# A gated unit beside attention on one core: how the two row halves of TensorE swap their halves of h

## The chip, the cores and the metric

One core of a Trainium2 chip. A kernel's time is the device time of one execution in microseconds (us); what is compared is the median over several executions. The engines are TensorE (PE, with its weight loads shown as PEld), VectorE (DVE), ScalarE (ACT), GpSimd (POOL) and SyncE (SP). In this kernel SP does nothing but issue DMA transfers, in the order in which the program hands them to it. A PE matmul writes its sums to PSUM, in banks of 128 x 512 float32; everything else lies in SBUF, 128 partitions wide.

## The reference

x has 2048 rows of 576. Attention with 32 heads of 18 columns, times the silu of a bilinear gated unit with F = 4608 inner columns, plus x:

```python
xn  = layernorm(x)                       # (2048, 576)
q, k, v = heads(xn @ wqkv)               # 32 heads, Dh = 18
p   = softmax(q @ k.T * Dh ** -0.5)      # per head, 2048 x 2048
s   = merge(p @ v) @ wo
h   = (xn @ w_gate) * (xn @ w_up)        # (2048, 4608)
g   = silu(h @ w_down)
out = x + s * g
```

All of it is float32. Where the kernel needs more than one pass of the array gives, a number is split in a high part (rounded to the type that PE multiplies fast, float32r) and a low part (the number less its high part), and a product takes three matmuls: high x high, high x low, low x high.

## The kernel before

A prologue (to about 194 us) normalises x and makes q, k and v. An end (from about 2502 us) multiplies by wo and writes the output. Between them lies the main stage, of which the change touches a part.

**Two streams on two halves of the array.** In the main stage the 128 rows of PE's array are used as two halves of 64 rows, and two matmuls that name different halves run beside each other. Stream 0 (rows 0 to 63) and stream 1 (rows 64 to 127) each hand out matmuls of the gated unit; scores of the attention are put between them, and the products with v (L639, float32, the whole array) come in 74 "visits", each of which stops both streams. Two passes are made over the scores: pass a (L596) for the row maximum, which DVE takes (L598), and pass b (L628), whose scores ACT turns into exponentials `pt` (L630). Pass b has two PSUM banks, `pb`. Pass a has two, `pa`. The unit and the visits share four, `pg`.

**The gated unit** is cut into 72 units u = (c, q): c is one of four chunks of 512 rows of x, q one of 18 groups of 256 inner columns. The 18 units of a chunk are called a sweep here. A unit has two products j = 0, 1 of 128 columns each, numbered n = 2u + j. Stream 0 computes up (27 matmuls of 512 columns, L675) and ACT copies it to SBUF (`us`, L680, in `up_end`). Stream 1 computes gate, and DVE multiplies the two in `gate_end` (L687): `us` now holds h of 128 inner columns for 512 rows. ACT rounds it to the high part `hs` (L690), POOL takes the low part (L691).

**The exchange.** The down product of the unit sums over 256 inner columns: each stream makes one half of the 576 output columns and needs all inner columns, but a stream's matmuls read only the 64 partitions of their own half. So each half needs the other half's h on its own partitions: `turn_round` moves the parts `hs` of one half to the partitions of the other, as `hx`, with two DMAs of 512 KB for a unit (L709). Then down takes 4 blocks of 128 rows, each 12 matmuls of 288 columns (L719, in the order of `DTERMS`: for j = 0 three with `hs` and three with `hx`, then the same for j = 1), and DVE adds the block to `acc` (L747, in `down_end`). `hx` has one buffer: the exchange for unit u+1 can only be issued when the last L719 of unit u has read `hx`. `down_end` does that when both streams have ended the unit: it calls `d_get(u + 1)`, which loads or prepares the next down weights, and then `turn_round(u + 1, 1)`. For unit 0 and the last two units `gate_end` calls `turn_round` itself; there the last unit but one has a buffer of its own, `hxl`.

**The weights.** In the first sweep they come from memory as they are, and are split on the way: "chores" round a piece on ACT (L193 for the gate and up weights `wgu`, L226 for the down weights `wd`), take the low part on POOL (L194, L227), store the split tile for later (L199, L232, 1152 KB each) and issue the loads of the raw weights ahead (L116, L124). In the later sweeps `wgu` and `wd` are loaded ready split (L185, L220, 1152 KB each). SP also issues the loads of q and k (L245, `ring` and `pair`), of v (L584) and, at the end, of the attention rows (o<-sot).

**What sets the order.** The program is unrolled, and a planner (`order`) writes it out when the kernel is built. It keeps a clock for each stream and times at which DVE, ACT and POOL come free; `can_go` says if a stream's next matmul may go, by the tables `there`, `downed`, `loaded`, `upped` and `gated`. `moved(start, size)` estimates when a transfer of so many MB lands, as one queue of 0.24 MB/us plus 2.0 us. Every engine's instructions then run on the chip in the order in which the planner wrote them, and an instruction that has to wait holds up all that stand behind it on its engine.

## Time and profile before

| | before |
|---|---|
| median of 3 runs | 2568.7 us (2567.2 to 2570.92) |
| the profiled execution's own time | 2567.59 us |
| its span in the profile | 2565.8 us |
| L675, gate and up matmuls | 7776, of 388 ns |
| L596 and L628, scores on half arrays | 2006 and 2005, of 393 and 395 ns |
| L630, exponentials on ACT | 2048, of 597 ns |

The profile shows one execution. Its times are in us from the span's start. A row of the list of groups names the line, the engine, the operation, what is written and read, the count, then the busy sum and the mean duration of one in ns. Matmuls on the two half arrays overlap, so their durations add to more than the span. A row of the waits names who waited on whom, then the sum, the count and the longest. A row of the timeline begins with the start and the duration; in square brackets stands how long the engine had been idle, and what ended it. SPq is the time that SP takes to issue a DMA. A row of the table of stretches gives the stretch, its length and the busy time (with the number of instructions) of PE, PEld, DVE, ACT, POOL and SPq, then the mean granted clock, the busy share of the DMA engines, and GB/s.

### The profile page before, as it was taken

Reading aid. Unit: us, or ns where it says so; the run is one execution under the profiler, and the core shown is the slowest. Engines: PE = TensorE matmul, PEld = TensorE weight load, DVE = VectorE, ACT = ScalarE, POOL = GpSimd, SP = SyncE. Lnnn points to the kernel's source line nnn. Section 1 sums busy time; section 2 is a strip of 40 time slices with the busy share of each in tenths; the row PEclk is TensorE's granted clock in tenths of the full one; section 3 lists DMA queues with packets and bytes.
Section 4 is the critical chain, followed back from the end, with each engine's and each line's share of the span. In section 5 each row is a group of like instructions: output and inputs, shape, how many; then the busy total and the mean of one; then the engine's idle time right before and its main releaser. Section 6 shows DMA issues by size and latency. Waiting matters only on the chain.

```text
span 2565.8 us, 59206 instructions
## 1 busy us (share of the span) xinstructions
PE 2544.8 (99%) x24360; PEld 2106.5 (82%) x24360; DVE 1931.5 (75%) x3377; ACT 1465.2 (57%) x2688; POOL 593.3 (23%) x663
## 2 busy tenths in 40 slices
PE   8999999999999999999999999999999999999999
PEld 7899888878878888878888888887888888878879
DVE  6208778777778898777778888777888887877537
ACT  5222666666756665655565666555665655555651
POOL 3214334433421111111111111111111111111125
PEclk9999999999999999999999999999999999999999
DMA  7799988888886666565676666665676666664577
GB/s 248 233 283 279 259 227 226 233 222 224 221 193 187 176 180 180 172 182 168 181 186 171 179 175 185 179 166 169 180 192 166 178 184 178 175 177 145 154 203 253
DMA packets 196058, 504.58 MB, mean 197 GB/s; under 512 B 58144, under 2 KB 116384, under 8 KB 156876
## 3 DMA queue, kind: packets, MB, share of 16 engines
q1 hardware_dynamic: 185100, 487.58, 68.2%
q0 software_dynamic: 9952, 11.74, 1.7%
q8 instruction: 192, 3.15, 0.6%
q10 hardware_dynamic: 736, 1.47, 0.2%
q14 instruction: 78, 0.64, 0.1%
HBM read 312.21 MB, written 107.61 MB: 164 GB/s over the span
## 4 chain that ended last, share of the span: by engine, by line
PE 97%; DVE 1%; DMA 1%; SPq 0%; issue 0%; ACT 0%; POOL 0%; DVEq 0%
PE pg L675 34%; PE pg L639 17%; PE pg L719 16%; PE pa L596 12%; PE pb L628 8%; PE pg L402 2%; PE pa L348 2%; PE pb L348 2%; PE pg L1243 1%; PE pa L1243 1%; PE pb L1243 1%; DMA hx<-hs 0%; DMA ring<-sqk 0%; DVE mx L598 0%; DMA xin<-in_A_x_dram 0%; DMA sot<-oc 0%
## 5 line engine op out<-in xcount | busy, mean ns | idle before, releaser
L598 DVE TENSOR_REDUCE mx<-pa 128x1 f32<-128x512 f32 x2048 | 1368.9, 687 | 226.1 <-PE pa L596 113.1
L630 ACT ACTIVATE pt<-pb 128x512 f32<-128x512 f32 x2048 | 1160.8, 597 | 538.2 <-PE pb L628 463.5
L675 PE MATMUL pg<-xc,wgu 64*128 64x512 f32 x7776 | 1363.9, 388 | 0.2 <-DVE acc L747 0.2
L675 PEld LDWEIGHTS pg<-xc,wgu 64*128 64x128 f32 x7776 | 1049.4, 184 | 41.4 <-DVE acc L747 0.5
L628 PE MATMUL pb<-pair,ring 64*128 64x512 f32 x2005 | 780.8, 395 | 2.3 <-DMA ring<-sqk 2.3
L596 PE MATMUL pa<-pair,ring 64*128 64x512 f32 x2006 | 777.3, 393 | 1.8 <-DVE mx L598 1.8
L719 PE MATMUL pg<-wd,hs 64*128 64x288 f32 x3408 | 585.1, 293 | 2.4 <-DVE acc L747 2.4
L719 PE MATMUL pg<-wd,hx 64*128 64x288 f32 x3360 | 572.4, 293 | 2.0 <-DMA hx<-hs 2.0
L719 PEld LDWEIGHTS pg<-wd,hs 64*128 64x128 f32 x3408 | 491.8, 185 | 7.1 <-DVE acc L747 2.8
L691 POOL TENSOR_TENSOR hs<-us,hs 128x512 fp32r<-128x512 f32 x144 | 185.9, 1291 | 1315.7 <-ACT hs L690 1301.6
L719 PEld LDWEIGHTS pg<-wd,hx 64*128 64x128 f32 x3360 | 480.4, 185 | 5.6 <-DMA hx<-hs 2.3
L639 PE MATMUL pg<-pt,vt 128*32 128x512 f32 x4096 | 455.8, 595 | 0.8 <-DVE acc L747 0.6
L596 PEld LDWEIGHTS pa<-pair,ring 64*128 64x128 f32 x2006 | 364.8, 184 | 70.7 <-issue 52.8
L628 PEld LDWEIGHTS pb<-pair,ring 64*128 64x128 f32 x2005 | 364.2, 184 | 9.3 <-issue 2.7
L639 PEld LDWEIGHTS pg<-pt,vt 128*32 128x32 f32 x4096 | 125.6, 110 | 285.1 <-issue 280.0
L747 DVE TENSOR_TENSOR acc<-acc,pg 128x288 f32<-128x288 f32 x544 | 234.0, 446 | 21.1 <-PE pg L719 20.1
L645 DVE TENSOR_TENSOR oc<-oc,pg 128x512 f32<-128x512 f32 x69 | 47.1, 683 | 216.6 <-PE pg L639 213.0
L690 ACT ACTIVATE hs<-us 128x512 fp32r<-128x512 f32 x144 | 91.0, 632 | 149.6 <-DVE us L687 148.0
L194 POOL TENSOR_TENSOR wgu<-wraw,wgu 128x384 fp32r<-128x384 f32 x108 | 108.4, 1015 | 97.3 <-ACT wgu L193 81.3
L643 ACT ACTIVATE oc<-pg 128x512 f32<-128x512 f32 x32 | 19.1, 598 | 184.9 <-PE pg L639 184.9
L687 DVE TENSOR_TENSOR us<-pg,us 128x512 f32<-128x512 f32 x144 | 98.4, 683 | 29.0 <-PE pg L675 22.3
L618 POOL DMA_DIRECT2D pair<-mt x128 | 77.6, 612 | 166.6 <-DVE mt L613 162.5
(143 smaller groups left out, 1366.5 us busy)
## 6 DMA issues: line engine op xcount, KB each, us to landing
wgu<-swg SPq DMA_DIRECT2D x102, 1152.0 KB
hx<-hs SPq DMA_DIRECT2D x140, 512.0 KB
wd<-swd SPq DMA_DIRECT2D x50, 1152.0 KB
swg<-wgu SPq DMA_DIRECT2D x36, 1152.0 KB
pair<-sqk SPq DMA_DIRECT2D x192, 144.0 KB
ring<-sqk SPq DMA_DIRECT2D x384, 72.0 KB
swd<-wd SPq DMA_DIRECT2D x18, 1152.0 KB
sqk<-hl SPq DMA_DIRECT2D x32, 512.0 KB
```

The source lines that it names most:

```text
L194: nc.gpsimd.tensor_tensor(w[:, 9 + b:12 + b, :], raw[:, b:b + 3, :], w[:, b:b + 3, :].bitcast(FT), op=OP.subtract)
L348: nc.tensor.matmul(p, wq[b, a], xcs[c][:, e, :], start=n == 0, stop=n == len(PAIRS) - 1)
L596: nc.tensor.matmul(p, q[rows, t * 128:(t + 1) * 128], k[rows, c * 512:(c + 1) * 512], start=True, stop=True)
L598: nc.vector.tensor_reduce(mx[h][:, t, c:c + 1], p, axis=AX.X, op=OP.max)
L628: nc.tensor.matmul(p, k[rows, t * 128:(t + 1) * 128], q[rows, c * 512:(c + 1) * 512], start=True, stop=True)
L630: nc.scalar.activation(pt[t, c], p, AF.Exp, scale=scale)
L639: nc.tensor.matmul(p[32 * c:32 * c + 32, :], vt[h // 2][:, t, 6 * (h % 2):6 * (h % 2) + 32], pt[t, c], start=t == ts[0], stop=t == ts[-1])
L675: nc.tensor.matmul(ps, gw[n][half[r], a, :], xg[i][half[r], e, :], start=k == 0, stop=k == len(TERMS) - 1)
L687: nc.vector.tensor_tensor(h32, ps, h32, op=OP.mult)
L691: nc.gpsimd.tensor_tensor(hj[:, 1, :], h32, hj[:, 0, :].bitcast(FT), op=OP.subtract)
L719: nc.tensor.matmul(ps[:, 0:HALF], (hx if k else hs)[u][half[r], j, a, s * 128:(s + 1) * 128], dw[u][half[r], k, j, e, :], start=n == 0, st ...
L747: nc.vector.tensor_tensor(a, a, ps[:, 0:HALF], op=OP.add)
```

## The change

The exchange moves the float32 product instead of its two parts. `turn_round` now sends `us` itself, as one DMA of 128 KB for each j and each half (L707), into the place where the low part will stand. When it has landed, the new function `cross` rounds it on ACT to the high part (L711) and POOL replaces it by the low part (L712), the same two operations as L690 and L691. `down_end` calls `turn_round(u + 1, (0, 1))` ahead of `d_get(u + 1)` instead of behind it. In unit 0 and the last two units each j is sent by `gate_end`.

In the planner, `there["h", n]` (the whole exchange) becomes `there["h", n, j]`, and `there["o", n, j]` is added for a half's own h. `can_go` asks for each of the four parts where down begins to read it, where it asked for all of `hx` at the first matmul. `sent` is the time by which a product has left `us`, which an up product now also waits for. The list `crossing` holds each `cross` back until the estimated landing plus BEFORE (1.5 us) and until ACT is free. L719, L745 and L747 of the kernel before are L722, L748 and L750 in the changed one.

```diff
         def gate_end(n, ps):
...
-            h32 = us.pop(n)
+            h32 = whole_h[n] = us.pop(n)
             nc.vector.tensor_tensor(h32, ps, h32, op=OP.mult)
             g_get(n + 2)
             hj = hs[u][:, j]
             nc.scalar.activation(hj[:, 0, :], h32, AF.Copy)
             nc.gpsimd.tensor_tensor(hj[:, 1, :], h32, hj[:, 0, :].bitcast(FT), op=OP.subtract)
-            if u == 0 and j or u >= len(units) - 2:
-                turn_round(u, j)
+            if u == 0 or u >= len(units) - 2:
+                turn_round(u, (j,))
...
-        def turn_round(u, j):
+        def turn_round(u, js):
...
-            for r in range(2):
-                nc.sync.dma_start(hx[u][half[r], js].bitcast(FT), hs[u][half[1 - r], js].bitcast(FT))
+            for j in js:
+                h32 = whole_h.pop(2 * u + j)
+                for r in range(2):
+                    nc.sync.dma_start(hx[u][half[r], j, 1, :].bitcast(FT), h32[half[1 - r], :])
+
+        def cross(u, j):
+            high, low = hx[u][:, j, 0, :], hx[u][:, j, 1, :]
+            nc.scalar.activation(high, low.bitcast(FT), AF.Copy)
+            nc.gpsimd.tensor_tensor(low, low.bitcast(FT), high.bitcast(FT), op=OP.subtract)
...
+                    if u + 1 < len(units) - 2:
+                        turn_round(u + 1, (0, 1))
                     d_get(u + 1)
-                    if u + 1 < len(units) - 2:
-                        turn_round(u + 1, 1)
...
+        LATER, BEFORE = 0.5, 1.5
...
             if kind == "d":
-                return k or (there.get(("h", n), 1e9) <= now and (n < 1 or downed.get(n - 1, 1e9) <= now))
+                if k % 3 == 0 and k < 12:
+                    if there.get(("oh"[k // 3 % 2], n, k // 6), 1e9) > now:
+                        return False
+                return k or n < 1 or downed.get(n - 1, 1e9) <= now
...
+                if crossing and crossing[0][0] + max(0.0, free["ACT"] - now - 0.1) <= now:
+                    _, u, j = crossing.pop(0)
+                    cross(u, j)
+                    there["h", u, j] = engine("POOL", engine("ACT", now, 0.535) + 0.05, 1.29) + LATER
...
-                                    downed[n] = moved(max(parts[n]) + 0.3, 1.18) if (n + 1) % NF2 and n + 2 < len(units) else 0.0
                                     if n + 3 < len(units):
-                                        there["h", n + 1] = moved(max(parts[n]) + 1.0, 1.05)
+                                        for j in range(2):
+                                            sent[2 * n + 2 + j] = moved(max(parts[n]) + 0.3, 0.262)
+                                            crossing.append((sent[2 * n + 2 + j] + BEFORE, n + 1, j))
+                                    downed[n] = moved(max(parts[n]) + 1.0, 1.18) if (n + 1) % NF2 and n + 2 < len(units) else 0.0
...
```

Where this moves instructions, engine by engine. First SP in the first sweep, at the exchange that has the load of v ahead of it. Before:

```order
L199 DMA swg<-wgu 128x2304
L116 DMA wraw<-in_B_w_up_dram 64x9x128
L116 DMA wraw<-in_B_w_gate_dram 64x9x128
L584 DMA vt<-sv 128x16x38
L709 DMA hx<-hs 64x2048 x2
L232 DMA swd<-wd 128x2304
```

And now, at the same place:

```order
L199 DMA swg<-wgu 128x2304
L116 DMA wraw<-in_B_w_up_dram 64x9x128
L116 DMA wraw<-in_B_w_gate_dram 64x9x128
L584 DMA vt<-sv 128x16x38
L707 DMA hx<-us 64x512 x4
L232 DMA swd<-wd 128x2304
```

Two transfers have become four smaller ones, and what stands ahead of them is the same. ACT at that place, before:

```order
L226 ACTIVATE wd<-draw 128x2x288
L630 ACTIVATE pt<-pb 128x512 x2
L226 ACTIVATE wd<-draw 128x2x288
L630 ACTIVATE pt<-pb 128x512 x3
L680 ACTIVATE us<-pg 128x512
L630 ACTIVATE pt<-pb 128x512 x2
L690 ACTIVATE hs<-us 128x512
```

And now:

```order
L226 ACTIVATE wd<-draw 128x2x288
L630 ACTIVATE pt<-pb 128x512 x2
L226 ACTIVATE wd<-draw 128x2x288
L630 ACTIVATE pt<-pb 128x512 x2
L711 ACTIVATE hx<-hx 128x512
L630 ACTIVATE pt<-pb 128x512
L680 ACTIVATE us<-pg 128x512
L711 ACTIVATE hx<-hx 128x512
L630 ACTIVATE pt<-pb 128x512 x2
L690 ACTIVATE hs<-us 128x512
```

The two L711, one for each product j, stand between exponentials, one of them ahead of the copy of up. In a later sweep SP had the load of the next down weights (L220) ahead of the exchange:

```order
L245 DMA ring<-sqk 18x1024 x3
L584 DMA vt<-sv 128x16x38
L220 DMA wd<-swd 128x2304
L709 DMA hx<-hs 64x2048 x2
L185 DMA wgu<-swg 128x2304
```

And now:

```order
L245 DMA ring<-sqk 18x1024 x3
L584 DMA vt<-sv 128x16x38
L707 DMA hx<-us 64x512 x4
L220 DMA wd<-swd 128x2304
L185 DMA wgu<-swg 128x2304
```

The exchange has moved ahead of that load. Last, PE at the end of the main stage, from the last visit (L639) on. Before, where the names `hs` and `hxl` are a unit's own and exchanged parts of h:

```order
L639 MATMUL pg<-pt,vt 32x512 x16
L719 MATMUL pg<-wd,hxl 128x288 x5
L719 MATMUL pg<-wd,hs 128x288 x6
L719 MATMUL pg<-wd,hxl 128x288 x6
L719 MATMUL pg<-wd,hs 128x288 x6
```

And now, where `wdl` and `hx` belong to the last unit:

```order
L639 MATMUL pg<-pt,vt 32x512 x16
L722 MATMUL pg<-wd,hxl 128x288 x3
L722 MATMUL pg<-wd,hs 128x288 x3
L722 MATMUL pg<-wd,hxl 128x288 x3
L722 MATMUL pg<-wd,hs 128x288 x3
L722 MATMUL pg<-wd,hxl 128x288 x3
L722 MATMUL pg<-wd,hs 128x288 x3
L722 MATMUL pg<-wd,hxl 128x288 x3
L722 MATMUL pg<-wd,hs 128x288 x3
L722 MATMUL pg<-wd,hxl 128x288 x3
L722 MATMUL pg<-wdl,hs 128x288 x6
```

Rows with x6 are pairs of three on the two halves, rows with x3 run on one half alone. Behind the last visit 179 matmuls of the down product stood before, and 123 stand now.

More of the change, by code (lines that the diff above doesn't have):

```diff
@@ L662, in finish @@
                 store(c, nc.gpsimd if h < H - 1 else nc.sync)
-        hs, us = {}, {}
+        hs, us, whole_h = {}, {}, {}
         TERMS = [t for b in range(9) for t in ((b, b, 0), (9 + b, b, 0), (b, b, 1))]
@@ L691, in gate_end @@
             nc.gpsimd.tensor_tensor(hj[:, 1, :], h32, hj[:, 0, :].bitcast(FT), op=OP.subtract)
-            if u == 0 and j or u >= len(units) - 2:
-                turn_round(u, j)
+            if u == 0 or u >= len(units) - 2:
+                turn_round(u, (j,))
         hx = {}
-        def turn_round(u, j):
-            if u >= len(units) - 2:
-                if j == 0 and u == len(units) - 2:
+        def turn_round(u, js):
+            if js[0] == 0:
+                if u == len(units) - 2:
                     hx[u] = accp.tile([128, 2, 2, 512], FR, name="hxl", tag="acc")
-                elif j == 0:
+                else:
                     hx[u] = gp.tile([128, 2, 2, 512], FR, name="hx", bufs=1)
-                js = slice(j, j + 1)
-            else:
-                hx[u] = gp.tile([128, 2, 2, 512], FR, name="hx", bufs=1)
-                js = slice(0, 2)
-            for r in range(2):
-                nc.sync.dma_start(hx[u][half[r], js].bitcast(FT), hs[u][half[1 - r], js].bitcast(FT))
+            for j in js:
[6 more added lines that the diff above has]
+            nc.gpsimd.tensor_tensor(low, low.bitcast(FT), high.bitcast(FT), op=OP.subtract)
         DTERMS = [(k, j, a, e) for j in range(2) for k in range(2) for a, e in ((0, 0), (0, 1), (1, 0))]
@@ L918, in moved @@
             return queue[0] + 2.0
-        due, rows_done = [], {}
+        due, rows_done, crossing, sent = [], {}, [], {}
         there, queue = {}, [0.0]
@@ L1087, in can_go @@
                     return False
-                if not r and n > 1 and gated.get(n - 2, 1e9) > now + 0.3:
+                if not r and n > 1 and max(gated.get(n - 2, 1e9), sent.get(n - 2, 1e9)) > now + 0.3:
                     return False
@@ L1176, in order @@
                             fin = engine("POOL", fin + 0.05, 1.29)
+                            there["o", n // 2, n % 2] = fin + 0.1
                             loaded[n] = moved(done - 0.4, 1.18) if (n // 2 + 1) % NF2 else 0.0
-                            if n // 2 >= len(units) - 2:
-                                there["h", n // 2] = moved(fin, 0.524) - (0.0 if n // 2 < len(units) - 1 else 1.1)
-                            elif n == 1:
-                                there["h", 0] = moved(fin, 1.05)
+                            if n < 2 or n // 2 >= len(units) - 2:
+                                sent[n] = moved(done + 0.5, 0.262)
+                                crossing.append((sent[n] - (0.8 if n == 2 * len(units) - 1 else 0.0), n // 2, n % 2))
                             for _ in range(2):
```

## The prediction

> **What bounds the kernel now.** I read the page first, then the list of who waits for whom, then short pieces of the timeline around the exchange. The busy times on the page, and the chain of work that ended last:
> ```profile
> PE 2544.8 (99%) x24360; PEld 2106.5 (82%) x24360; DVE 1931.5 (75%) x3377; ACT 1465.2 (57%) x2688; POOL 593.3 (23%) x663
> ...
> PE 97%; DVE 1%; DMA 1%; SPq 0%; issue 0%; ACT 0%; POOL 0%; DVEq 0%
> ```
> TensorE (PE) sets the time. The change takes no matmul away and adds none, so it can move the time only through PE's waits and through how well the two row halves are paired. PE's own waits, apart from those of the prologue:
> ```profile
> PE pg L719 <- DVE acc L747: 2.4, 1, 2.4
> PE pb L628 <- DMA ring<-sqk: 2.3, 1, 2.3
> ...
> PE pg L719 <- DMA hx<-hs: 2.0, 1, 2.0
> ...
> PE pa L596 <- DVE mx L598: 1.8, 3, 0.8
> ```
> They come to 8.5 us. Only one, of 2.0 us, is for the exchange (hx<-hs). So the **ceiling of the gain is 8.5 us**, a third of a per cent, and what the change plainly aims at is 2. There is no such ceiling on a loss.

> **The change, part by part.** Matmuls: the same number of each kind, so nothing.

> The new rounding and splitting (L711 on ScalarE, L712 on GpSimd in the changed kernel) are the same operations as L690 and L691, on the same shape, once more for each of 144 halves of a product:
> ```profile
> L690 ACT ACTIVATE hs<-us 128x512 fp32r<-128x512 f32 x144 | 91.0, 632 | 149.6 <-DVE us L687 148.0
> L691 POOL TENSOR_TENSOR hs<-us,hs 128x512 fp32r<-128x512 f32 x144 | 185.9, 1291 | 1315.7 <-ACT hs L690 1301.6
> ```
> ACT gets 144 x 0.632 = 91 us (57% becomes 61%), POOL 144 x 1.291 = 186 us (23% becomes 30%). Both have idle time for it and the exponentials are placed around it, so the work itself costs nothing. If that cover went, ACT's 91 us would reach PE through L630, since only two PSUM buffers (pb) stand between a score and its exponential.

> The transfer: 2 x 512 KB for a unit become 4 x 128 KB. In an otherwise empty queue:
> ```profile
> 413.39 0.29 PE L719 MATMUL pg<-wd,hx 64*128 64x288 f32 x1
> ...
> 413.80 1.15 SPq L709 DMA_DIRECT2D hx<-hs  x2
> ```
> ```profile
> 413.00:414.80 1.80, 1.80 (x22) 1.61 (x20) 1.46 (x4) 1.80 (x5) 0.93 (x1) 1.00 0.00 0
> 414.80:420.40 5.60, 5.60 (x54) 5.24 (x52) 4.96 (x8) 4.62 (x9) 3.85 (x4) 1.00 0.99 227
> ```
> The last hx read ends at 413.68, SP issues 0.12 later at 0.57 us each, and the DMA engines (last columns: busy share, GB/s) start 1.0 us after the issue and take 5.6. Half the bytes would take 2.8, and the first product's share is half of that: it is there about 0.12 + 1.0 + 1.4, and at the latest 0.12 + 1.1 + 1.0 + 0.6, so some 3 us after the last read. The order puts the first L711 about 5 us of PE work behind that read (counted in matmuls at the spacing of the timeline's rows). Two microseconds to spare: **where the queue is empty, nothing is lost.** From the second sweep on that is so, since the load of the next down's weights (L220, 1152 KB), which stood ahead of the exchange, now stands behind it. That load has 20 us until its use and loses only some 2 us by the exchange ahead of it: nothing. No row shows how fast descriptors of 2048 bytes are, a quarter of the old ones. At one end they cost their bytes, as taken here. At the other each takes as long as one of 8192, and then the first product lands 0.12 + 1.0 + 5.6 = 6.7 us after the read, 1.7 late, everywhere. The page counts the packets of the whole span:
> ```profile
> DMA packets 196058, 504.58 MB, mean 197 GB/s; under 512 B 58144, under 2 KB 116384, under 8 KB 156876
> ```
> Over half are under 2 KB, and the mean is still 197 GB/s, near the 227 above. So I take the first, and keep the other as a rival.

> The new wait: L711 stands in ACT's queue and waits for a landing, and everything behind it on ACT waits too: exponentials (L630), the up eviction (L680). In the first sweep (194 to about 720 us) SP is not free when the down ends: it still issues the store of split weights and two raw loads, in order. Three places, by the old order in the timeline. First:
> ```profile
> 285.18 0.29 PE L719 MATMUL pg<-wd,hx 64*128 64x288 f32 x1
> ...
> 286.42 2.72 SPq L584 DMA_DIRECT2D vt<-sv  x1
> ...
> 289.23 5.46 SPq L709 DMA_DIRECT2D hx<-hs  x1
> ...
> 290.34 0.60 ACT L630 ACTIVATE pt<-pb 128x512 f32<-128x512 f32 x1 [0.54 <-PE pg L675]
> ```
> [...] The new SP order has the same rows here. In ACT's new order L711 follows the exponential that starts at 290.34 here, so its slot is near 290.9. The landing of the first product needs the issue of two DMAs and their transfer: 289.2 + 5.5 + 0.6 + about 2 = 297.3. ACT stands for 6.4 us, and the exponential behind it comes that much later. The two pb buffers are refilled every 0.7 to 1.1 us here, so PE can go on for about 0.5 us: I take **+6**.

> Second place, one unit earlier:
> ```profile
> 256.58 0.29 PE L719 MATMUL pg<-wd,hx 64*128 64x288 f32 x1
> ...
> 263.62 2.28 SPq L709 DMA_DIRECT2D hx<-hs  x2
> 264.04 0.60 ACT L680 ACTIVATE us<-pg 128x512 f32<-128x512 f32 x1 [3.37 <-PE pg L675]
> ...
> 274.53 0.39 PE L719 MATMUL pg<-wd,hx 64*128 64x288 f32 x1 [2.04 <-DMA hx<-hs]
> ```
> This is the stall for hx. The landing comes 10.9 us after the issue. Of the changed transfer, the first quarter should be there some 5 us after it, at 268.8. L711 now stands just ahead of L680, which would run at 264.0, and so ACT waits about 5 us and PE some 4.5 of them. In return PE is later at hx than the split product (near 273) and the old stall of 2.3 goes: **+2.2**.

> Third:
> ```profile
> 644.36 0.29 PE L719 MATMUL pg<-wd,hx 64*128 64x288 f32 x1
> ...
> 645.46 0.34 SPq L199 DMA_DIRECT2D swg<-wgu  x1
> ...
> 648.03 1.67 SPq L709 DMA_DIRECT2D hx<-hs  x2
> ```
> The exchange is issued 3.4 us after the last read, behind a store of 1152 KB and two loads of 288 KB. At the 227 GB/s above these 1.77 MB, queued from 645.5 on, take until 653.3, and the first product lands past 653.5, at least 3.8 us behind L711's slot (five after the read, 649.7). I counted eight of the first sweep's seventeen exchanges issued over 1.5 us late. In the new order most of them have a visit of the value product (L639) behind L711, in which ACT has nothing to do and the wait is free. One such place in the open I take at **+3**; three where only the queue is late at 0.3 each, **+1**. Bounds: 0, if exponentials have slack that I don't see, and 8 x 4 = 32, if no visit covers any.

> The end. PE behind the last visit:
> ```profile
> 2483.34 3.67 PE pg L639 x32
> 2487.03 0.70 DVE oc L645
> ...
> 2491.49 10.48 PE pg L719 x145
> ```
> DVE finishes the last head from 2487.03 on, and only then empties the bank that PE wants at 2491.49. The old order has 179 L719 behind the visit, the new one 123, the first 27 of them all on one half: 27 x 0.13 = 3.5 us fill the stall but for 1.1, and 96 at 10.48 / 145 = 0.072 take 6.9. That is 4.65 + 6.9 = 11.6 where 15.1 were. The 56 others now run ahead of the visit, 56 x 0.072 = 4.0, and halves without a partner cost some 1 us more there (the larger half's sum over all stretches between visits, less the mean). The attention rows for the last product (o<-sot) are now all issued behind the last head's store, of which I take 0.5: **+2**, between -2.6 and +4.

> [...]
> ```profile
> L655 DVE TENSOR_TENSOR tp<-tp,rc x32: 457/459/1552, 393.1 to 2488.8; 128x288 f32<-128x288 f32 x32
> ```
> One of 32 took 1.55 us for 0.46, the one at 2488.79. [...]

> Sum: 6 + 2.2 + 3 + 1 + 2 = 14.2 on the profiled execution's 2567.59 us, which gives 2581.8. That execution is 1.1 below the median of the three runs (2568.7), inside their spread, so I predict **2582**.

> **Rivals.** (a) *The waits are covered.* If L711 comes late enough or exponentials have room, the places cost nothing, the stall for hx goes (-2.3) and the end costs 2: 2567.3, no change. For it: ACT is idle 43% of the time. Against it: L711 is queued in front of exponentials that PE needs within 0.5 us. (b) *The lighter queue ends PE's DMA waits*, faster: hx 2.3 and the ring rows at 755.8 (2.3) both wait on a queue that half the exchange leaves, and the 27 matmuls fill the stall at 2488.8 (2.4): 2567.6 - 7.0 = 2560.6. It decides if no L711 waits over 0.5 us in the open. Against it: the ring wait is at the change of a chunk, where other loads fill the queue. (c) *L711 waits in later sweeps too*, if a descriptor of 2048 bytes takes as long as one of 8192: 1.7 us of wait, 1.2 of them PE's, at some 50 exchanges give +60, 2642. That the change doesn't do what it says I leave out: the order shows L707 ahead of L220.

> **How the numbers follow.** My case 0.58 (2573 to 2598, by the bounds of the places in the first sweep), (a) 0.25, (b) 0.12, (c) 0.05. Over 0.2% means over 5.1 us, about what can be told from no change. My case and (c) give 0.62 for slower, but for the edge of mine (0.01); (a) 0.25 for the same, (b) and that edge 0.13 for faster. The range takes in (a) and my case, and leaves out (c), most of (b) and 0.02 at the top of mine: 2562 to 2598.

> **What will show it.** Right: ACT waits at L711 for DMA hx<-us, few but of 3 to 6 us, nearly all before 720 us, with PE waits of the same size at L628 behind ACT's L630; no L711 wait after 900 us. PE's wait for hx gone; a wait for DVE's finish near the end of about 1 us instead of 2.4. Wrong: L711 hardly waits for a DMA (then a or b), or waits in every sweep (c), or PE's added time lies behind DVE or POOL.

## The result, and the profile after

| | before | changed |
|---|---|---|
| median | 2569.3 us (2567.2 to 2570.9, 5 runs) | 2625.8 us (2623.3 to 2629.0, 5 runs) |
| span of the profiled execution | 2565.8 us | 2621.5 us |
| mean granted clock | 0.999 | 0.992 |

The ratio is 1.0222, with a 95% interval from 1.021 to 1.0233. The changed kernel is slower by 56 us, where 13 were forecast and the range ended at 29.

The busy times and the chain that ended last, from the page of the changed kernel:

```profile
PE 2566.0 (98%) x24360; PEld 2111.5 (81%) x24360; DVE 1933.4 (74%) x3377; ACT 1523.6 (58%) x2832; POOL 778.3 (30%) x807
...
PE 92%; DMA 4%; DVE 2%; issue 1%; ACT 1%; POOL 1%; SPq 0%; ACTq 0%; POOLq 0%; DVEq 0%
```

DMA has come into the chain with 4%. PE's busy time has also grown, by 21 us with the same 24360 matmuls; part of this is matmuls that ran slower, as the granted clock below shows. PE's waits apart from the prologue's, from the list of waits:

```profile
PE pb L628 <- ACT pt L630: 33.9, 11, 10.6
...
PE pa L596 <- DVE mx L598: 2.9, 6, 0.7
PE pg L639 <- DVE acc L750: 1.3, 1, 1.3
```

The wait for hx is gone, and PE now waits for exponentials. What ACT itself waited for, between 194 and 900 us and then between 900 and 2470:

```profile
ACT hx L711 <- DMA hx<-us: 60.5, 12, 13.9
ACT us L680 <- DMA hx<-us: 10.4, 2, 6.8
```
```profile
ACT hx L711 <- DMA hx<-us: 8.5, 7, 2.5
```

So the new wait is where the prediction put it, in the first sweep, and it reaches PE in the way described. It is larger: PE waits 33.9 us for exponentials, where the terms of the sum have 14.5. The largest place in the timeline:

```profile
258.05 0.42 PE L722 MATMUL pg<-wd,hx 64*128 64x288 f32 x2
...
260.55 1.08 ACT L630 ACTIVATE pt<-pb 128x512 f32<-128x512 f32 x2
262.77 0.34 SPq L199 DMA_DIRECT2D swg<-wgu  x1
...
265.45 0.61 SPq L116 DMA_DIRECT2D wraw<-in_B_w_up_dram  x1
...
266.86 4.42 SPq L707 DMA_DIRECT2D hx<-us  x4
276.10 0.63 ACT L711 ACTIVATE hx<-hx 128x512 fp32r<-128x512 f32 x1 [13.89 <-DMA hx<-us]
...
278.27 0.79 PE L628 MATMUL pb<-pair,ring 64*128 64x512 f32 x1 [10.55 <-ACT pt L630]
```

The last read of hx ends at 258.5. SP still has a store and two loads of weights to issue and comes to the exchange at 266.9, and L711 runs at 276.1, 9.2 us after that. ACT has stood since 262.2 with exponentials queued behind, and PE loses 10.6 us. The table of stretches at this place (the columns are PE, PEld, DVE, ACT and POOL, then the granted clock, the DMA share and GB/s):

```profile
264.00:267.50 3.50, 3.50 (x28) 3.08 (x24) 1.38 (x2) 0.00 (x0) 0.00 (x0) 1.00 0.94 282
267.50:278.20 10.70, 0.21 (x1) 0.00 (x0) 0.96 (x2) 2.10 (x5) 1.40 (x2) 0.60 1.03 309
278.20:283.20 5.00, 4.93 (x24) 3.85 (x26) 2.40 (x4) 2.74 (x7) 5.00 (x5) 0.50 0.55 132
283.20:288.20 5.00, 5.00 (x51) 4.33 (x49) 3.26 (x6) 2.79 (x6) 0.23 (x1) 1.00 0.79 240
```

In the 5 us after the wait PE counts as busy but does 24 matmuls where the next 5 us hold 51: the granted clock is 0.50. A part of the stall is paid a second time.

To see where the time went, I compare the start of each visit (the first L639 of 74 groups, which both kernels have). The rows say how much later than in the kernel before each kernel reaches it; the end is that of the last matmul. The names are those of the experiments below.

| us later than before at visit | 1st | 10th | 15th | 18th | 70th | 74th | end |
|---|---|---|---|---|---|---|---|
| (time in the kernel before) | 299 | 572 | 723 | 820 | 2396 | 2483 | 2562 |
| changed kernel | 17.5 | 33.1 | 46.7 | 45.9 | 48.8 | 55.4 | 54.6 |
| late_half | 13.6 | 29.3 | 42.4 | 38.5 | 40.9 | 53.5 | 50.2 |
| late_cross | 2.1 | 7.5 | 11.8 | 5.0 | 10.2 | 15.1 | 27.8 |
| late_sent | 4.6 | 12.7 | 16.2 | 6.8 | 12.3 | 17.5 | 41.7 |
| pool_round | 19.0 | 22.1 | 39.1 | 35.1 | 35.4 | 47.4 | 43.8 |
| pool_queue | 11.9 | 24.6 | 43.0 | 40.3 | 43.1 | 50.1 | 49.8 |
| swap_issue | 18.8 | 34.4 | 47.9 | 50.4 | 156.1 | 175.8 | 174.3 |
| old_end | 17.2 | 33.0 | 46.4 | 45.9 | 48.8 | 55.0 | 53.6 |
| old_first | -1.7 | -1.5 | -0.7 | -3.3 | -0.4 | 12.0 | 8.0 |
| old_both | -0.9 | -0.7 | 0.1 | -2.1 | 0.5 | 8.6 | 7.5 |
| act_hold | 1.6 | 1.6 | 1.6 | -0.8 | 59.1 | 59.2 | 59.0 |

The changed kernel loses 46 us by the 18th visit, 3 in the 52 visits behind it, and 6 at the end. The value of a single visit moves by a microsecond or two, since a visit may stand a little sooner or later in the order. In late_cross and late_sent it moves by far more: a visit is reached there with less of the streams' work done, which is then left for the end. So I also add up, from 194 us to the 19th visit, how long PE stood, what its matmuls lost to a lowered clock ((1 - granted clock) over the time that PE was busy), and how many matmuls fewer than in the kernel before were done by then.

| 194 us to the 19th visit | before | changed | late_half | late_cross | late_sent | pool_round |
|---|---|---|---|---|---|---|
| PE stood, us | 5.3 | 37.7 | 32.8 | 10.0 | 17.0 | 28.9 |
| lost by the clock, us | 3.4 | 12.7 | 9.3 | 5.9 | 2.5 | 11.2 |
| matmuls fewer than before | | 7 | 7 | 124 | 222 | 0 |

### The profile page after: what moved, and what is told of

Read it like the earlier page. It is cut to its first block, busy times and chain, and to the rows that moved or that the text cites. A ratio compares the mean times of both kernels' runs of the same rounds, so it can differ in the third digit from the quotient of the medians.

```text
span 2621.5 us, 60144 instructions
## 1 busy us (share of the span) xinstructions
PE 2566.0 (98%) x24360; PEld 2111.5 (81%) x24360; DVE 1933.4 (74%) x3377; ACT 1523.6 (58%) x2832; POOL 778.3 (30%) x807
## 4 chain that ended last, share of the span: by engine, by line
PE 92%; DMA 4%; DVE 2%; issue 1%; ACT 1%; POOL 1%; SPq 0%; ACTq 0%; POOLq 0%; DVEq 0%
PE pg L675 33%; PE pg L639 17%; PE pg L722 15%; PE pa L596 11%; PE pb L628 8%; DMA hx<-us 3%; PE pg L402 2%; PE pa L348 2%; PE pb L348 2%; PE pg L1256 1%; PE pb L1256 1%; DVE mx L598 1%; PE pa L1256 1%; DMA sqk<-hl 0%; DMA wraw<-in_B_w_gate_dram 0%
## 5 line engine op out<-in xcount | busy, mean ns | idle before, releaser
L598 DVE TENSOR_REDUCE mx<-pa 128x1 f32<-128x512 f32 x2048 | 1368.1, 688 | 253.0 <-PE pa L596 150.2
L630 ACT ACTIVATE pt<-pb 128x512 f32<-128x512 f32 x2048 | 1151.5, 597 | 473.6 <-PE pb L628 426.4
L675 PE MATMUL pg<-xc,wgu 64*128 64x512 f32 x7776 | 1399.2, 390 | 1.3 <-ACT wgu L193 1.0
L675 PEld LDWEIGHTS pg<-xc,wgu 64*128 64x128 f32 x7776 | 1064.8, 186 | 47.9 <-ACT wgu L193 1.3
L628 PE MATMUL pb<-pair,ring 64*128 64x512 f32 x2020 | 791.2, 398 | 33.3 <-ACT pt L630 33.2
L596 PE MATMUL pa<-pair,ring 64*128 64x512 f32 x2006 | 781.6, 395 | 2.9 <-DVE mx L598 2.9
L722 PE MATMUL pg<-wd,hs 64*128 64x288 f32 x3408 | 566.7, 292 | 1.4 <-DVE acc L750 1.2
L722 PE MATMUL pg<-wd,hx 64*128 64x288 f32 x3360 | 556.0, 292 | 0.0
L722 PEld LDWEIGHTS pg<-wd,hs 64*128 64x128 f32 x3408 | 471.0, 185 | 7.4 <-DVE acc L750 2.3
L722 PEld LDWEIGHTS pg<-wd,hx 64*128 64x128 f32 x3360 | 457.3, 185 | 3.5 <-POOL wd L227 0.3
L639 PE MATMUL pg<-pt,vt 128*32 128x512 f32 x4096 | 455.1, 594 | 1.3 <-DVE acc L750 1.3
L596 PEld LDWEIGHTS pa<-pair,ring 64*128 64x128 f32 x2006 | 366.6, 185 | 74.0 <-issue 54.5
L628 PEld LDWEIGHTS pb<-pair,ring 64*128 64x128 f32 x2020 | 368.7, 185 | 48.8 <-ACT pt L630 41.9
L691 POOL TENSOR_TENSOR hs<-us,hs 128x512 fp32r<-128x512 f32 x144 | 186.3, 1294 | 632.4 <-ACT hs L690 626.9
L712 POOL TENSOR_TENSOR hx<-hx 128x512 fp32r<-128x512 f32 x142 | 181.7, 1292 | 630.8 <-ACT hx L711 470.3
L639 PEld LDWEIGHTS pg<-pt,vt 128*32 128x32 f32 x4096 | 125.7, 110 | 284.5 <-issue 279.4
L750 DVE TENSOR_TENSOR acc<-acc,pg 128x288 f32<-128x288 f32 x544 | 237.9, 447 | 32.7 <-PE pg L722 25.6
L645 DVE TENSOR_TENSOR oc<-oc,pg 128x512 f32<-128x512 f32 x69 | 47.2, 684 | 219.4 <-PE pg L639 210.9
L690 ACT ACTIVATE hs<-us 128x512 fp32r<-128x512 f32 x144 | 91.0, 632 | 138.2 <-DVE us L687 138.0
L194 POOL TENSOR_TENSOR wgu<-wraw,wgu 128x384 fp32r<-128x384 f32 x108 | 108.2, 1014 | 106.9 <-ACT wgu L193 105.8
L711 ACT ACTIVATE hx<-hx 128x512 fp32r<-128x512 f32 x142 | 88.9, 634 | 70.1 <-DMA hx<-us 69.9
```

What stands on the lines that cost most here:

```text
L194: nc.gpsimd.tensor_tensor(w[:, 9 + b:12 + b, :], raw[:, b:b + 3, :], w[:, b:b + 3, :].bitcast(FT), op=OP.subtract)
L596: nc.tensor.matmul(p, q[rows, t * 128:(t + 1) * 128], k[rows, c * 512:(c + 1) * 512], start=True, stop=True)
L598: nc.vector.tensor_reduce(mx[h][:, t, c:c + 1], p, axis=AX.X, op=OP.max)
L628: nc.tensor.matmul(p, k[rows, t * 128:(t + 1) * 128], q[rows, c * 512:(c + 1) * 512], start=True, stop=True)
L630: nc.scalar.activation(pt[t, c], p, AF.Exp, scale=scale)
L639: nc.tensor.matmul(p[32 * c:32 * c + 32, :], vt[h // 2][:, t, 6 * (h % 2):6 * (h % 2) + 32], pt[t, c], start=t == ts[0], stop=t == ts[-1])
```

## The experiments

**Where ACT stands: the rounding ordered later.** In the run late_cross one constant is changed for the first sweep, so that L711 is ordered 8 us later; late_half does the same with 3 us.

```diff
-crossing.append((sent[2 * n + 2 + j] + BEFORE, n + 1, j))
+crossing.append((sent[2 * n + 2 + j] + (9.5 if n + 1 < NF2 + 3 else BEFORE), n + 1, j))
```

> The changed kernel, with one number of the planner changed: in the first sweep (units 1 to 20) the rounding and splitting of the landed copy (L711, L712) are ordered 8 us later, so that they stand behind the landing in ACT's queue. Theory: what costs the time is that L711 stands in ACT's in-order queue ahead of its landing and holds up exponentials; then L711's 60 us of waiting before 900 us fall under 10, PE's 33.9 us of waiting at L628 for L630 under 5, and the half-clock pieces behind them go: 2578 to 2592 us. Rival 'late landing': the parts come late wherever they are rounded, down starts later, and PE waits at L722 or the streams run out of work: 2605 us or more, with new PE waits at L722. Rival 'extra work' (ACT's 89 us and POOL's 182 us are themselves what costs): no change from 2626.

> The run with the later rounding again, with 3 us more instead of 8 (4.5 us behind the estimated landing in units 1 to 20). Theory: L711's waits in the first sweep were 1.3 to 13.9 us, with half of them under 4.6; 3 us take away the short ones and shorten the long ones, so that the first sweep's 47 us of loss become 15 to 30 and PE's L628 waits under 20 us. Behind the 70th visit the longer half's matmuls add to 75.1 us in this order (76.2 before, 78.7 in the changed kernel, 86.6 with 8 us more), so the end should cost no more than in the kernel before: 2582 to 2599 us.

late_cross took 2594.1 us (ratio 1.0098, 1.0084 to 1.0112), just above the 2592 expected. Up to the 19th visit PE stands 10.0 us instead of 37.7, and the clock costs 5.9 instead of 12.7: most of the waits are gone. So the bulk of the loss is not in the added work, which is all still there. The 5 us at the 18th visit flatter this run, since 124 matmuls are still to be done, some 12 us by the 51 in 5 us of the stretch above (an estimate). Behind the 70th visit it loses another 18 us, part of them in a wait of PE itself at 2520.8 for a rounded copy, with 3.1 us by the clock behind it:

```profile
PE pg L722 <- ACT hx L711: 5.8, 1, 5.8
```

This is the kind of wait that the rival named, though not in its place, and the time stays under the rival's 2605. late_half missed: 2621.9 us (1.0203, 1.0187 to 1.0218), with 38.5 of the 46 us left and 32.2 us of PE's waits at L628, where less than 20 were expected. ACT's waits between 194 and 900 us, first in late_half, then in late_cross:

```profile
ACT us L680 <- DMA hx<-us: 49.0, 10, 14.4
ACT hx L711 <- DMA hx<-us: 19.6, 6, 7.3
```
```profile
ACT us L680 <- DMA hx<-us: 23.6, 7, 8.6
ACT hx L711 <- DMA hx<-us: 8.3, 2, 5.4
```

With 3 us more, L711's waits fell from 60.5 to 19.6, and those of L680 rose from 10.4 to 49.0. This is a second wait on the same landing, which the prediction did not have: `us` has two buffers, the exchange now reads `us` itself, and so the next copy of up may not start before the exchange is through. In the kernel before only the split on ACT and POOL read `us` behind the product, and from 194 to 2500 us L680 waited for PE alone (23.8 us). Both waits stand in ACT's queue, ahead of exponentials. Why L680 waits less with 8 us more than with 3 no run separates: the constant moves PE's own order too.

**The same rounding on another engine.** In pool_round GpSimd rounds the landed copy, so that no L711 stands on ACT:

```diff
-            nc.scalar.activation(high, low.bitcast(FT), AF.Copy)
+            nc.gpsimd.tensor_copy(high, low.bitcast(FT))
             nc.gpsimd.tensor_tensor(low, low.bitcast(FT), high.bitcast(FT), op=OP.subtract)
```

> The changed kernel with the rounding of the landed copy on GpSimd instead of ScalarE (L711 as a copy on POOL, right ahead of L712), planned so. Theory (ACT's queue is what couples the landing to PE): no ACT wait for hx<-us is left but those of L680 for the buffer us, PE's L628 waits fall under 8 us, and POOL waits for the landing instead, 40 us or more in the first sweep; 2580 to 2592. Rival 'any in-order engine will do': POOL's weight splitting (L194, L227) is held up as the exponentials were, and PE waits at L675 or L722 for POOL instead: 2605 to 2625.

It took 2610.5 us (1.0164, 1.015 to 1.0178): the theory's 2592 is missed, and the time lies in the rival's range. The waits show whether it is so for the rival's reason. From the list of waits, over the whole span:

```profile
POOL hx L711 <- DMA hx<-us: 253.8, 42, 15.5
...
ACT us L680 <- DMA hx<-us: 43.0, 10, 14.4
...
PE pb L628 <- ACT pt L630: 29.3, 8, 10.3
```

POOL stands 253.8 us for the exchange, and no wait of PE for a split weight (L194, L227) is among the listed ones, so the rival's mechanism does not show: GpSimd could stand that long without PE waiting for it. The theory had L680's wait but not its size, and so PE's 29.3 us at L628, where less than 8 were expected. What is left is again L680 on ACT.

**Both waits of ACT together.** In late_sent the planner takes the exchange itself to land 5 us later in the first sweep, which moves L711 and L680 both.

```diff
-sent[2 * n + 2 + j] = moved(max(parts[n]) + 0.3, 0.262)
+sent[2 * n + 2 + j] = moved(max(parts[n]) + 0.3, 0.262) + (5.0 if n + 1 < NF2 + 3 else 0.0)
```

> The changed kernel in which the planner takes the exchange of units 1 to 20 to land 5 us later than it did (the entry sent), so that both of the instructions that hang on it move: L711, and the next copy of up (L680), which may not overwrite us before the exchange has read it. Theory (after the run with 3 us more, where L680's waits took the place of L711's): both waits of ACT for hx<-us together fall under 20 us before 900 us, from 70 in the changed kernel, PE's L628 waits under 10, and the visits up to the 15th come within 12 us of the kernel before, where they were 47 late. The longer half's matmuls add to 8 us more than in the kernel before, nearly all behind the 70th visit: 2577 to 2590 us. Rival (some other wait turns up in its place, on PE at L722 or on DVE): the 15th visit is 25 us late or more, and the time 2600 or more.

By the 18th visit it is 6.8 us late, where the changed kernel is 45.9; the 15th was 16.2 late, a little over the 12 expected. ACT's two waits came to 37.3 us before 900 us (23.4 and 13.9), above the 20 expected, and PE's at L628 to 12.2, of which 10 were expected. The total, 2610.4 us (1.016, 1.0145 to 1.0176), missed: another 24 us are lost behind the last visit. Part of that is work put off: PE was 222 matmuls behind at the 19th visit, and 148 more than before stand behind the last one. The other part, 7.8 us, is 5.4 us more in which PE stood and 2.4 by the clock, with one wait at 2535.6 for the rounding:

```profile
PE pg L722 <- ACT hx L711: 5.0, 1, 5.0
```

So the rival was right in part: a wait at L722 did turn up, at the end and not in the first sweep.

**Is it the place in the queue?** In pool_queue the stores L199 and the raw loads L116 of the first sweep are issued by GpSimd, so that SP is free for the exchange; PE's order is the same.

```diff
-            nc.sync.dma_start(swg[f], w.bitcast(FT))
+            (nc.gpsimd if started else nc.sync).dma_start(swg[f], w.bitcast(FT))
```

> The changed kernel with the stores of the split gate and up weights (L199) and the raw loads (L116) of the first sweep issued on GpSimd's queue instead of SP's; PE's order is the same. Theory 'place in the queue' (the exchange lands late because SP issues it behind a store of 1152 KB and two loads of 288 KB): it lands some 4 us sooner, L711's waits before 900 us fall from 60 us under 25, and the time to 2590 to 2605. Rival 'busy DMA engines' (the bytes are the same and every queue shares the engines): within 5 us of 2626. Third: GpSimd is held up by its own DMA issues and PE waits for it instead (L675 for L194): over 2635.

One run took 2617.6 us, 8 less than the changed kernel. That lies between the two theories, above the 2605 of the first and below the rival's 2621. ACT's waits from 194 to 900 us (two lines have been added ahead, L711 is L713 here and L680 is L682):

```profile
ACT hx L713 <- DMA hx<-us: 52.9, 14, 7.8
ACT us L682 <- DMA hx<-us: 3.4, 1, 3.4
```

The longest wait fell from 13.9 to 7.8, but the sum only from 70.9 to 56.3. So SP's place accounts for a part, the longest waits above all. The rest stays when another queue carries the weights. That fits the rival, by which the exchange shares busy DMA engines with them (0.94 to 1.03 of the time in the first two rows of the stretches above), but no run tests it by itself. The third possibility showed a little: PE waited 5.4 us for split gate and up weights (L195 and L196 here), against 1.3 in the changed kernel.

**What a stall costs.** act_hold is the kernel before, with ACT held up in the later sweeps, at twelve places that the planner does not know of:

```diff
-            nc.scalar.activation(us[n], ps, AF.Copy)
+            for _ in range({44: 4, 52: 8, 60: 14, 68: 6, 76: 10, 84: 4, 92: 8, 100: 14, 108: 6, 116: 10, 124: 5, 132: 12}.get(n, 1)):
+                nc.scalar.activation(us[n], ps, AF.Copy)
```

> The kernel before, with ScalarE held up on purpose at twelve places of the later sweeps: at every fourth unit from 22 on, the first copy of up (L680) is written 4, 8, 14, 6, 10, 4, 8, 14, 6, 10, 5, 12 times instead of once, the same values each time; the planner does not know. One more copy is 0.6 us, so ACT is held 1.8, 4.2, 7.8, 3.0, 5.4, 1.8, 4.2, 7.8, 3.0, 5.4, 2.4, 6.6 us, 53.4 in all. Theory (two pb banks cover some 1 us; a PE wait of 3 us and more is followed by some 5 us at a granted clock of 0.5, a price of about 2.5 on top, a wait under 2 us by none): waits of 41 us and 7 x 2.5 for the clock, about +58 us. Rival 'no price beyond the wait': +41. Rival 'covered' (the planner's slack takes most of it up): +20 or less.

One run took 2626.6 us, 57 more than the median before, and its visits came 59 us late: the theory's 58. One place of it, ACT's rows and then PE's in the table of stretches:

```profile
1147.28 8.78 ACT L681 ACTIVATE us<-pg 128x512 f32<-128x512 f32 x14
1155.96 1.08 ACT L630 ACTIVATE pt<-pb 128x512 f32<-128x512 f32 x2
```
```profile
1149.50:1156.50 7.00, 0.16 (x1) 0.00 (x0) 0.89 (x2) 6.68 (x13) 0.00 (x0) 0.80 0.30 66
1156.50:1161.00 4.50, 4.40 (x22) 3.48 (x24) 1.98 (x3) 2.47 (x6) 1.19 (x1) 0.55 0.43 131
1161.00:1166.00 5.00, 5.00 (x50) 4.42 (x50) 3.80 (x6) 3.30 (x7) 0.10 (x1) 1.00 0.43 166
```

Thirteen copies more, 8.2 us, made PE wait 6.9, and 4.5 us at a clock of 0.55 followed. All places, with the clock's loss as (1 - granted clock) added up behind the wait:

| unit | 22 | 26 | 30 | 34 | 38 | 42 | 46 | 50 | 54 | 58 | 62 | 66 |
|---|---|---|---|---|---|---|---|---|---|---|---|---|
| copies more | 3 | 7 | 13 | 5 | 9 | 3 | 7 | 13 | 5 | 9 | 4 | 11 |
| PE's wait, us | 0 | 3.8 | 6.9 | 2.3 | 5.1 | 1.0 | 3.1 | 1.9 | 2.1 | 4.9 | 1.7 | 6.3 |
| lost by the clock, us | 0 | 3.0 | 2.0 | 1.7 | 1.4 | 0 | 3.1 | 0 | 1.7 | 1.6 | 1.7 | 2.5 |

The waits add to 39 us and the clock to 19, together 58 of the 60 us that are lost between the 18th and the 70th visit. At unit 50 a visit covers most of the hold. So a third of the price of these stalls was the clock.

**The issue ahead of the weights.** In swap_issue only the two calls in `down_end` are put back in the old order; the planner still counts on the new one, and PE's order is that of the changed kernel.

```diff
-                    if u + 1 < len(units) - 2:
-                        turn_round(u + 1, (0, 1))
                     d_get(u + 1)
+                    if u + 1 < len(units) - 2:
+                        turn_round(u + 1, (0, 1))
```

> The changed kernel with only the issue put back: the load of the next down's weights (L220) ahead of the exchange (L707), with the planner's times left as they are, so that PE's and ACT's orders are those of the changed kernel. In the later sweeps the exchange then lands behind 1152 KB, some 5 us later. If the prediction's two microseconds to spare there are right, L711 waits about 3 us at most of some 50 exchanges, and PE 1 to 2.5 us of each where no visit covers it: 2670 to 2740 us, with half-clock pieces behind the longest. Rival (transfers share the DMA engines rather than queue, or ACT's slack takes it): 2626 to 2640. The first sweep stays as it is.

One run took 2743.9 us, just above the 2740 at which the expectation ended. Between the 18th and the 70th visit it loses 106 us, where the changed kernel loses 3. From its waits:

```profile
PE pb L628 <- ACT pt L630: 117.3, 48, 10.5
...
ACT hx L711 <- DMA hx<-us: 111.8, 31, 13.8
ACT us L680 <- DMA hx<-us: 91.1, 28, 7.3
```

The margin of the later sweeps is small, as the prediction had it: the load of 1152 KB (L220) between the last read of hx and the exchange on SP is enough to use it up.

**Parts of the change put back.** old_end has the old exchange for the last two units, old_first for the first sweep, old_both for both. For the first sweep this stands in `turn_round`; for the last two units `gate_end` issues the two DMAs of each `hs` itself, as in the kernel before.

```diff
+            if u < FIRST_NEW:
+                for j in js:
+                    whole_h.pop(2 * u + j)
+                for r in range(2):
+                    nc.sync.dma_start(hx[u][half[r]].bitcast(FT), hs[u][half[1 - r]].bitcast(FT))
+                return
```

> The changed kernel with the last two units alone exchanged as before (both parts hs, two DMAs for each product, no L711 and L712 there). Between the 70th visit and the end the changed kernel loses 5.8 us against the kernel before. Theory: that comes from the last two units' new exchange (a wait of ACT for the last landing at 2535, and the order around it): it goes, 2618 to 2622 us. Rival: it comes from elsewhere in the new order, for instance the attention rows for the last product issued behind the last head's store: 2624 to 2628.

> The changed kernel with the old exchange (both parts hs, two DMAs of 512 KB, no L711 and L712) for the 18 units of the first sweep, and the new one from unit 18 on. Theory (the loss sits in the first sweep, where L711 is ahead of its landing; the new exchange of the later sweeps gives and takes nothing): no L711 wait over 0.3 us before 740 us, PE's stall of about 2 us for hx at 274 as in the kernel before, the visits up to the 70th within 3 us of the kernel before, and the end by its pairing (the longer half's matmuls behind the 70th visit add to 74.1 us against 76.2 before): 2565 to 2574 us. Rival 'the later sweeps cost as well' (ACT's and POOL's added work, 2048-byte descriptors): 2578 or more.

> The new exchange in the units 18 to 69 alone; the first sweep and the last two units swap both parts hs as before. In the run with only the first sweep put back the 70th visit came 0.4 us before that of the kernel before, and the end lost 8.4 us, 4.3 of them in one wait of PE at L628 behind the copy L680, which waited for hx<-us. Theory: the last two units' exchange is the cause there; without it the end loses 0 to 4 us: 2567 to 2574 us. Rival: the end loses as much as before for the order's sake: 2576 to 2581.

old_end took 2624.7 us (1.022, 1.0206 to 1.0234): the theory fell, since 5 of the 6 us at the end are lost without the new exchange there too. old_first took 2579.3 us (1.0041, 1.0029 to 1.0054), over the 2574 expected and in the rival's range, but not for the rival's reason. Up to the 70th visit it is as good as the kernel before, as expected, with PE's old stall for the exchange back:

```profile
PE pb L628 <- ACT pt L630: 4.3, 1, 4.3
...
PE pg L729 <- DMA hx<-hs: 2.0, 2, 1.6
```

It lost 8 us at the end, which was not expected; the wait of 4.3 us is there, at 2486.7. old_both took 2575.6 us (1.0028, 1.0017 to 1.0038), nearer to the rival than to the theory: that wait fell to 2.3, but the end still costs 7 us. These are 4.2 us more in which PE stood and 2.8 by the clock: besides the 2.3 there are three waits of 2.8 in all, in the last product, for the rounded attention rows. No version beats the kernel before.

## Why the prediction was wrong

**What bounds the kernel, and the ceiling of the gain:** right in kind. The stall for hx went, and no more than the stalls could have been won. The ceiling itself was low: rows of under 1 us in the same list add 1.0 to the 8.5, and the clock had cost 3.4 behind two of the waits.

**The added work costs nothing:** right, to within what a visit's place moves. old_both has it in 52 units, and from the 18th to the 70th visit it loses 2.6 us against the kernel before.

**Where the queue is empty, nothing is lost:** right for PE. The sign "no L711 wait after 900 us" did not hold: there were seven, up to 2.5 us and 8.5 in all. None of them shows as a wait of PE for an exponential. The landing came as it was worked out: by the DMA packets in the trace, over 48 exchanges between 900 and 2470 us, the first 128 packets of 2048 bytes, as many as a product has, were through 2.5 us after the first issue in the median, where the prediction had 2.4. Such a packet took 0.15 us there, and the median packet of 8192 bytes in the whole trace 0.50. So rival (c), which gave 2642 us and came nearest in time, is wrong in its condition too, and not only in putting its waits into every sweep.

**The first sweep:** right in the mechanism, wrong in the size. The prediction had 12.2 us; the first 18 visits lost 46. The stretches up to the 19th visit, in the kernel before and in the changed one:

```profile
194.00:853.30 659.30, 654.01 (x6450) 540.94 (x6452) 523.81 (x907) 406.26 (x766) 244.04 (x245) 0.99 0.86 227
```
```profile
194.00:900.00 706.00, 668.27 (x6444) 539.29 (x6447) 525.05 (x908) 423.89 (x808) 296.16 (x286) 0.97 0.73 196
```

PE stood 5.3 us before and 37.7 after, 32.4 more. Behind five of the waits the clock was halved, with a loss of 2.5, 3.2, 2.9, 2.3 and 1.7 us (added up as in act_hold), 12.7 where the kernel before has 3.4: 9.3 more. These two make 41.7 of the 47 us by which the second stretch is longer; the other 5 I cannot assign. Against the terms of the sum:

| place in the prediction | PE's wait, forecast | PE's wait, measured | clock, measured |
|---|---|---|---|
| the value load (L584) between, 289 us | 6 | 3.1 at 307.5 | 3.2 |
| one unit earlier, 263 us | 4.5 | 10.6 at 278.3 | 2.5 |
| behind a store and two loads, 648 us | 3 | 2.0 at 687.1 | 0 |
| the others | 1 | 18.2 at seven places | 7.0 |

Three steps failed. First, "three where only the queue is late at 0.3 each", and the view that a visit covers most of the others. PE waited 1.0, 1.5, 1.0, 4.8, 5.8 and 3.1 us there (343.6, 409.7, 514.6, 581.1, 725.7, 798.1; with 1.0 more at 751.8 for a weight that ACT rounds). The one at 798.1 was L680's wait for `us`, a wait that the sum did not have at all. Second, the landing at 263 us was set "some 5 us after" the issue, from a transfer in the old trace; it took 9.2, and the issue itself came 8.4 us behind the last read, where it had been 6.8. At this place too a store and two loads of weights stand ahead of the exchange (L199 and L116 in the timeline above); the prediction counted their bytes at 648 us, and not here. Third, a stall was counted at its own length. The bound of 32 us for this sweep was built from 4 us a place, and so held neither the place with 10.6 nor the clock.

**The end:** sized +2, and 5.8 us were measured from the 70th visit on. In the planner's order the matmuls of the longer half, added up over the stretches behind that visit to the end, come to 2.5 us more (78.7 against 76.2). PE stands no longer there (2.4 us in both), but the clock costs 1.7 more, behind waits of 0.7 and 1.0 us in the last product. The stall for DVE's finish went whole, where some 1 us of it was forecast to stay. That the end costs nearly as much with the old exchange there (old_end, old_both) points at the planner's order at the end, and not at the exchange. The remaining 1.6 us, and why that order is worse than the old one, stay open.

**The row of L655:** it was read too narrowly. In the kernel before, five of the 32 L655 and not one were long, with 0.80 to 1.55 us where the median is 0.46, and each began while GpSimd ran a L691 or L834. In the changed kernel it is four, with 0.69 to 1.40 us, begun during a L691, a L837 and in one case a L712 (1.07 at 2506.1). Of the short ones none began during arithmetic of GpSimd before, and two in the changed kernel, in the last 0.13 us of a L712 and the last 0.05 of a L194. But 185 us more of POOL (778.3 for 593.3) brought no more long rows, and no wait of PE shows for one. That GpSimd is what makes them long no run tests by itself.

## What to carry to other kernels

Before an instruction that waits for a transfer is put into an engine's queue, look at what stands behind it and at the transfer's landing in the busiest stage, not in an empty queue: here the same edit cost 3 us in 52 visits and 46 in 18. Moving such a wait is no cure while a second instruction of the same queue hangs on the same transfer, such as the copy that needs its source buffer back. And a stall of TensorE can be dearer than its length, as the waits of act_hold were, 39 us with 19 more by the clock: look at the granted clock behind each stall of the old trace before pricing a new one. When a change of order is judged by the time at which marks are reached, count as well how much work was done by then.

## What the runs showed of the hardware

Behind some waits of PE the granted clock was 0.50, and it stayed there for a while after the work had come back: in the changed kernel from 269.6 to 283.2 us, with the wait of 10.6 us ending at 278.3. All twelve waits of 3 us and more in the main stage of the changed kernel and of act_hold were followed by such a loss, of 1.4 to 3.2 us each. The kernel before had it too, behind the stall of 2.04 us that the prediction quotes: the clock was 0.50 from 275.2 to 278.6 us there, 1.7 us lost, and this was not read.

```profile
271.73:275.15 3.42, 1.38 (x15) 1.13 (x14) 0.69 (x1) 1.56 (x3) 0.00 (x0) 1.00 1.00 304
275.15:278.56 3.41, 3.41 (x28) 3.41 (x26) 2.34 (x4) 1.72 (x3) 0.50 (x1) 0.50 0.77 269
```
```profile
406.95:410.36 3.41, 1.57 (x14) 1.15 (x11) 1.86 (x3) 0.04 (x1) 0.37 (x1) 1.00 1.16 230
410.36:413.78 3.42, 1.78 (x16) 1.47 (x18) 0.75 (x2) 2.94 (x6) 2.03 (x2) 1.00 1.04 405
413.78:417.19 3.41, 3.41 (x34) 2.79 (x32) 3.17 (x6) 2.25 (x5) 0.56 (x1) 1.00 0.89 208
```

The stall of 2.04 us falls into one step, and the next is at 0.50. That of 3.48 us is cut into 1.84 and 1.64, and nothing follows. From 194 to 2500 us of the kernel before and of the changed one, PE stood 1.84 us or more in seven steps at full clock, and each was followed by one at 0.50; in the others it stood 1.34 us or less, and none was. This is a count and no limit: 1.84 us was not followed in late_sent, and 0.77 (at 250.8 in late_cross) and 1.11 (256.2 in old_both) were. What sets these apart is not shown.
